# Moving the product of batch 0's last token row to other PSUM banks and an earlier place, and output copies behind the attention work, in a fused linear-attention and SwiGLU kernel

## The chip, the cores and the metric

The kernel runs on one core of a Trainium2 chip. The metric is the device time of one execution in microseconds (us).

## The reference

Linear attention with the feature map phi(x) = elu(x) + 1 on 8 batches, 8 heads, 576 tokens and head size 64, then a SwiGLU block on the 4608 x 512 result:

```
k.v = phi(k)^T v        z = sum over tokens of phi(k)
x   = (phi(q) k.v) / (phi(q) z + 1e-6)
out = (silu(x w_gate) * (x w_val)) w_out        # 512 -> 1536 -> 512
```

The kernel treats the 4608 tokens as nine groups of 512. A batch has 576 tokens, nine rows of 64, so group 0 holds eight rows of batch 0, and group 1 holds the ninth row of batch 0 and seven rows of batch 1.

## The kernel before

Names used below. PE is the matmul engine, ACT is ScalarE, DVE is VectorE, POOL is GpSimd. The granted clock is the share of its full clock that PE was allowed, as the trace records it (1 is full). The kernel uses eight PSUM banks: pG[0..1], pV[0..2], pX[0..2]. Each second-layer step of group 0 accumulates in pV[0], pG[0], pV[1] or pG[1]; between these steps the program interleaves the attention of batch 1 in the other four banks.

The pieces that matter, cut from the kernel (line numbers of the kernel before in comments; dots mark cuts; the lambdas of the list are left out):

```
def corners(ps, lhs, b, j0, j1, lps=(0, 1)):          # L260: one 64x64 matmul for each head
    for lp in lps:
        for hh in range(2):
            for e in range(2): nc.tensor.matmul(out=ps[2*lp+e][C*hh:C*hh+C, :], ...)

dbank, nbank = (pX[0], pX[1]), (pX[2], pV[2])

def t1(lp): ...        # L743: transposes of phi(q) of batch 1 into pX[0] (lp 0) or pX[2] (lp 1),
                       # copied out by ACT (lp 0, L746) or DVE (lp 1, L748)
def den1(lp):
    corners({2*lp+e: dbank[e][:, 0:W7] for e in range(2)}, zs, 1, 0, 7, (lp,))   # denominators
    ln0([b[:, 0:W7] for b in dbank], rr[:, 2*lp:2*lp+2, 0:W7])                     # L655: ACT, ln
    exp_neg(rr[:, 2*lp:2*lp+2, 0:W7])                                              # L658: 1/den

num8_out = [pV[2][:, 0:C], pX[1][:, W7:W7+C], pV[2][:, C:2*C], pX[0][:, W7:W7+C]]
def num8(): corners(num8_out, kv(0), 0, 8, 9)      # batch 0's ninth row times its k.v: 8 matmuls
def x8():                                          # L661: DVE, four small scalings of it
    for m in range(4): x0(num8_out[m], r8[:, m % 2, part8[m]], xT[m][1][:, 0:C])

w = at(17, [    # (step i, what): issued behind the i-th piece of group 0's second layer
    (3, z0(1,0)), (3, z0(1,1)), (3, q_block), (7, t1(0)), (8, t1(1)),
    (8, den1(0)), (8, num8), (8, x8), (9, mm1(1,0)), (9, mm1(1,1)),
    (9, den1(1)), (9, r1_copies), (10, num1(0)), (10, x1(0)), (10, w_rest),
    (12, t2), (12, num1(1)), (12, x1(1)), (13, exp_k(2,0)), (13, den2), (14, num2), ... ])

for (i, (t, f0, f1)) in enumerate(...):            # the 16 pieces of the second layer
    ...
    l2(0, t, f0, f1)                               # L446
    if i > 11: l2_out(0, t, V)                     # L456: DVE copies a finished output tile
    for f in w[i]: f()
```

z0 (L626) is the key sum of batch 1, mm1 (L177) its k.v product, num1 its numerators, t2 (L753, copied by DVE in L755) the transposes of its last two rows and den2 and num2 what num1 and den1 are for these two rows. `num8` is the subject. Its even corners go to pV[2], its odd ones to columns 448 to 511 of pX[1] and pX[0]. Columns 0 to 447 of these two banks are `den1`'s.

## Time and profile before

| | before |
|---|---|
| median time (range), as given with the kernel | 307.1 us (306.84 to 307.11), 3 runs |
| PE busy, mean granted clock | 97%, 0.996 (full in the stage; the recorded loss is in the last 2.4 us of the span, behind the last matmul) |
| stage studied: first second-layer matmul of group 0 to first first-layer matmul of group 1 | 36.57 to 53.34 = 16.77 us |
| PE's longest wait in that stage | 1.24 us |

The page of the kernel before, its busy times and its chain of work that ended last:

```profile
PE 296.4 (97%) x2596; PEld 181.5 (59%) x2596; DVE 247.5 (81%) x526; ACT 193.4 (63%) x313; POOL 49.2 (16%) x61
...
PE 89%; issue 5%; DMA 2%; ACT 1%; DVE 1%; POOL 0%; POOLq 0%; DVEq 0%; ACTq 0%
```

PE bounds the kernel. But the busy share says little of what is left to gain: the Trainium skill, "Trainium Kernel Development and Optimization", section "Performance Expectations", calls matmul busy time a bad metric for the distance to roofline because matmuls are pipelined. What can be gained are gaps between matmuls on the chain.

The timeline of PE in the kernel before (start, duration, instruction, shapes, count, and in brackets the idle time before it and what ended it):

```profile
42.02 0.55 PE L743 MATMUL pX<-id,qp 128*128 128x128 f16 x7
42.50 0.38 PE L260 MATMUL pX<-qT,zz 64*64 64x448 f16 x4
42.72 0.19 PE L260 MATMUL pV<-qT,R 64*64 64x64 f16 x1
44.14 0.19 PE L260 MATMUL pX<-qT,R 64*64 64x64 f16 x1 [1.24 <-ACT rr L655]
...
44.32 1.04 PE L446 MATMUL pG<-wo,hT 128*128 128x512 f16 x4
```

den1(0) is issued at 42.50. num8's first matmul, into pV, follows at 42.72. The second, into pX, starts only at 44.14. Everything behind it on PE, above all four ready second-layer matmuls, stands in the queue. The ACT timeline shows what it waits for, the two ln of den1(0):

```profile
42.93 1.16 ACT L655 ACTIVATE rr<-pX,epst 128x448 f32<-128x448 f32 x2 [0.66 <-PE pX L260]
```

They end at 44.09. num8 does not use their result. It only writes other columns of the two banks that they read. The skill, "PSUM — Partial Sum Buffer", section "Terms", says that a matmul writing a bank quadrant while ScalarE or VectorE reads it is a collision error; so the program has to order the two. The trace shows that ordering as a wait, and shows the first corner, in a bank that ACT does not read, passing freely.

A second, smaller gap, from the chain of the kernel before in order of time (start, duration, piece):

```profile
49.93 0.05 DVE osb L456
49.98 0.55 issue
50.53 0.42 DVE qT L755
50.96 0.04 issue
51.00 0.30 PE pX L260 x7
```

den2 at 51.00 waits for DVE's copy of the transposes t2 (L755), and that copy stood behind an output copy (L456). PE's last matmul before it started at 50.50; with a normal step of the size PE would have been free about 0.2 us before 51.00.

### The profile page before, as it was taken

To read this page: it belongs to the slowest core of one execution; us is meant where nothing else is said; L and a number is where in the kernel's file an instruction comes from. 1 tells how busy PE (TensorE), PEld (TensorE's weight loads), DVE (VectorE), ACT (ScalarE), POOL (GpSimd) and SP (SyncE) were. 2 spreads that over 40 slices of the span, in tenths; PEclk is the share of its full clock that TensorE was granted. 3 is DMA by queue.
4 is the path that set the end of the run, shared out by engine and by line. 5 is a ranking of instruction groups with operands and counts; after the bars stand their busy time and mean duration, and the time that the engine had idled before them with its cause. 6 is when DMAs were issued, how large, how long until landed. Compare 5 with 4: busy or idle time off the path is not lost.

```text
span 305.5 us, 6677 instructions
## 1 busy us (share of the span) xinstructions
PE 296.4 (97%) x2596; PEld 181.5 (59%) x2596; DVE 247.5 (81%) x526; ACT 193.4 (63%) x313; POOL 49.2 (16%) x61
## 2 busy tenths in 40 slices
PE   8899989999999999999999999999999999999993
PEld 5644444444444486447644774467446888878883
DVE  4754647888868997998899878997999868968991
ACT  4874976947754588466855685468633478547931
POOL 8654254510001001100110000000000004001300
PEclk9999999999999999999999999999999999999998
DMA  7999999999589218931794133133312050033014
GB/s 205 193 196 201 206 207 215 195 209 195 112 166 155 52 28 182 184 58 29 159 185 78 29 72 69 27 54 69 72 26 54 12 129 0 2 68 72 2 37 103
DMA packets 41472, 32.88 MB, mean 108 GB/s; under 512 B 16400, under 2 KB 36816, under 8 KB 41440
## 3 DMA queue, kind: packets, MB, share of 16 engines
q0 software_dynamic: 20176, 18.35, 38.6%
q1 hardware_dynamic: 21104, 13.97, 19.8%
q8 instruction: 20, 0.33, 0.4%
q10 hardware_dynamic: 160, 0.13, 0.2%
q14 instruction: 12, 0.10, 0.1%
HBM read 37.75 MB, written 9.44 MB: 154 GB/s over the span
## 4 chain that ended last, share of the span: by engine, by line
PE 89%; issue 5%; DMA 2%; ACT 1%; DVE 1%; POOL 0%; POOLq 0%; DVEq 0%; ACTq 0%
PE pV L287 23%; PE pG L287 21%; PE pX L502 14%; PE pV L502 4%; PE pV L339 4%; PE pG L339 4%; PE pV L446 3%; PE pX L287 3%; PE pG L446 3%; DMA q<-in_q_dram 2%; PE pV L260 1%; PE pX L260 1%; PE pX L339 1%; PE pX L177 1%; PE pV L407 1%
## 5 line engine op out<-in xcount | busy, mean ns | idle before, releaser
L287 PE MATMUL pV<-xT,wv 128*128 128x512 f16 x324 | 83.5, 379 | 0.0
L287 PE MATMUL pG<-xT,wg 128*128 128x512 f16 x296 | 76.3, 379 | 0.0
L292 ACT ACTIVATE sil<-pG 128x512 f16<-128x512 f32 x74 | 43.5, 597 | 47.1 <-PE pG L287 32.2
L293 DVE SCALAR_TENSOR_TENSOR hT<-pV,sil 128x512 f16<-128x512 f32 x81 | 55.0, 687 | 15.2 <-PE pV L287 7.6
L287 PEld LDWEIGHTS <-wv 128*128 128x128 f16 x336 | 32.9, 98 | 39.6
L287 PEld LDWEIGHTS <-wg 128*128 128x128 f16 x336 | 32.3, 98 | 39.1 <-DVE xT L276 0.8
L502 PEld LDWEIGHTS <-hs 128*128 128x128 f16 x336 | 32.5, 98 | 4.7 <-DVE hs L476 0.4
L379 POOL TENSOR_TENSOR hT<-prod,vm 128x512 f16<-128x512 f16 x6 | 6.9, 1153 | 127.5 <-ACT vm L366 127.5
L502 PEld LDWEIGHTS <-hT 128*128 128x128 f16 x252 | 24.3, 98 | 4.1
L502 PE MATMUL pX<-ws,hs 128*128 128x256 f16 x210 | 25.7, 273 | 0.0
L507 ACT ACTIVATE part<-pX 128x256 f32<-128x256 f32 x35 | 12.8, 381 | 13.2 <-PE pX L502 13.1
L476 DVE TENSOR_TENSOR hs<-hT 128x512 f16<-128x512 f16 (+2 forms) x42 | 17.4, 417 | 0.2
L241 DVE TENSOR_TENSOR qp<-qp,rden 128x768 f16<-128x768 f16 x18 | 17.1, 948 | 0.0
L228 DVE TENSOR_REDUCE den<-prod 128x12 f32<-128x768 f16 x18 | 17.0, 942 | 0.0
L120 ACT ACTIVATE ek<-k 128x1152 f16<-128x1152 f16 x14 | 16.0, 1160 | 0.1
L95 POOL DMA_DIRECT2D k<-in_k_dram x7 | 5.2, 745 | 64.1 <-ACT part L507 44.0
L502 PE MATMUL pX<-wo,hT 128*128 128x256 f16 x126 | 15.2, 272 | 0.0
L130 DVE TENSOR_TENSOR kp<-kp,ek 128x1152 f16<-128x1152 f16 x14 | 10.6, 758 | 5.4 <-ACT ek L120 5.0
L446 PEld LDWEIGHTS <-hT 128*128 128x128 f16 x96 | 8.7, 98 | 10.1 <-issue 0.6
L151 ACT ACTIVATE vm<-v 128x1152 f16<-128x1152 f16 x12 | 14.1, 1175 | 0.0
L120 ACT ACTIVATE eq<-q 128x1152 f16<-128x1152 f16 x12 | 13.3, 1169 | 0.0
L512 DVE SCALAR_TENSOR_TENSOR osb<-pX,part 128x256 f32<-128x256 f32 x28 | 11.0, 418 | 2.1 <-PE pX L502 1.9
(186 smaller groups left out, 514.7 us busy)
## 6 DMA issues: line engine op xcount, KB each, us to landing
out_dram<-osb SPq DMA_DIRECT2D x64, 128.0 KB, 2.6
k<-in_k_dram POOLq DMA_DIRECT2D x7, 576.0 KB, 7.6
q<-in_q_dram POOLq DMA_DIRECT2D x7, 576.0 KB, 9.3
v<-in_v_dram POOLq DMA_DIRECT2D x7, 576.0 KB, 12.1
wg<-in_moe_w_gate_dram POOLq DMA_DIRECT2D x5, 256.0 KB, 8.9
wv<-in_moe_w_val_dram POOLq DMA_DIRECT2D x5, 256.0 KB, 9.5
wo<-in_moe_w_out_dram POOLq DMA_DIRECT2D x2, 512.0 KB, 15.1
out_dram<-osb SPq DMA_DIRECT2D x13, 64.0 KB, 2.0
```

The source lines that it names most:

```text
L120: nc.scalar.activation(out=e[:, s, :], in_=src[b % 2][:, s, :], func=AF.Exp, bias=0.0, scale=1.0)
L151: nc.scalar.activation(out=vm[b % 2][:, :, s, 0:D].rearrange("p j l d -> p l j d"), in_=v16[b % 2][:, s, :].rearrange("p l (j d) -> p l j ...
L228: nc.vector.tensor_reduce(out=den[:, HL * j0:HL * j1], in_=prod[:, 0:j1 - j0, :].rearrange("p j (l d) -> p (j l) d", d=D), axis=AX.X, op=A ...
L241: nc.vector.tensor_tensor(out=qv, in0=qv, in1=rden[:, HL * j0:HL * j1].unsqueeze(2).to_broadcast([P, HL * (j1 - j0), D]), op=ALU.mult)
L287: nc.tensor.matmul(out=ps[:, :], lhsT=src[:, i, P * fb:P * fb + P], rhs=xT[i][g % 2][:, :], start=(i == 0), stop=(i == 3))
L292: nc.scalar.activation(out=s[:, :], in_=pg[:, :], func=AF.Silu, bias=0.0, scale=1.0)
L293: nc.vector.scalar_tensor_tensor(out=hT[g % 2][:, fb, :], in0=pv[:, :], scalar=SC, in1=s[:, :], op0=ALU.mult, op1=ALU.mult)
L339: nc.tensor.matmul(out=dst[:, HN * e:HN * e + HN], lhsT=lhs, rhs=rhs, start=(n in (1, 2, 5) and e == 0 and c == 0), stop=(c == 1), skip_gr ...
L446: nc.tensor.matmul(out=pso[(g, t)][:, :], lhsT=hT[g % 2][:, fb, P * t:P * t + P], rhs=wo[:, fb, :], start=(fb == 0), stop=(fb == FB - 1))
L476: (eng or nc.vector).tensor_tensor(out=o, in0=a, in1=b, op=op)
L502: nc.tensor.matmul(out=(z if n in (2, 3, 5) else x)[:, 0:HD], lhsT=left(f), rhs=right(f), start=(f == 0 and n in (1, 2, 5)), stop=(f == HF ...
L507: nc.scalar.activation(out=part[:, 2 * i + tt, :], in_=(x if from_x else z)[:, 0:HD], func=AF.Copy, bias=0.0, scale=1.0 / SC)
```

## The change

The intent is to give num8 banks that nobody reads at the moment when it is issued, and to let PE go straight from den1(0) to second-layer matmuls while ACT takes the ln. num8 goes to step 3, in front of the key sums z0, into the free last 128 columns of the two banks of z0. Its scalings x8 go behind the q block. Apart from that, the output copies are issued behind the step's attention work.

```diff
-    num8_out = [pV[2][:, 0:C], pX[1][:, W7:W7 + C], pV[2][:, C:2 * C], pX[0][:, W7:W7 + C]]
+    num8_out = [(pX[2], pV[2])[m % 2][:, 3 * P:4 * P][:, part8[m]] for m in range(4)]
...
-            (3, lambda: z0(1, 0)), (3, lambda: z0(1, 1)), (3, q_block), (7, lambda: t1(0)), (8, lambda: t1(1)),
-            (8, lambda: den1(0)), (8, lambda: num8()), (8, lambda: x8()), (9, lambda: mm1(1, 0)), (9, lambda: mm1(1, 1)),
+            (3, lambda: num8()), (3, lambda: z0(1, 0)), (3, lambda: z0(1, 1)), (3, q_block), (3, lambda: x8()), (7, lambda: t1(0)), (8, lambda: t1(1)),
+            (8, lambda: den1(0)), (9, lambda: mm1(1, 0)), (9, lambda: mm1(1, 1)),
...
         l2(0, t, f0, f1)
+        for f in w[i]:
+            f()
         if i > 11:
             l2_out(0, t, V)
-        for f in w[i]:
-            f()
```

## The prediction

> **What bounds it.** The matmul engine (PE): the page gives 97% busy, 89% of the chain that ended last, granted clock 0.996. Busy time is a poor distance to the roofline (the Trainium skill, "Trainium Kernel Development and Optimization", Performance Expectations), so I looked for PE gaps. In the timeline of group 0's second layer (36.6 to 53.3 us) the last-row product num8 issues its first matmul, into pV, at 42.72; its second, into pX, starts only at 44.14. The waits view has PE pX <- ACT rr (ln), 1.24 us, PE's only listed wait there. The ln reads other columns of the same pX banks; the first matmul, in a bank that ACT does not read, went through. That agrees with the skill ("PSUM — Partial Sum Buffer", Terms): PE writing a bank while ScalarE reads it is a collision, so the program waits. It is in the chain ("ACT rr 1.16, issue 0.04").
>
> A small second gap: chain "DVE osb 0.05, issue 0.55, DVE qT 0.42, issue 0.04" before den2 at 51.00. PE would be free at about 50.82. The copy of the transposes stood behind an output copy (0.68 us, DVE).
>
> **The change.** It computes the same. num8's eight matmuls (0.18 us on PE) move to step 3, before z0, into columns 384 to 511 of pX[2]/pV[2], banks that z0 waits for there anyway. Its four scalings x8 (DVE, 0.61 us together) move behind the q block. Output copy 0 goes behind the transposes' copy and x1(1).
>
> **Walk of the new schedule** (estimates from the durations above):
> - PE after step 3 runs 0.2 us later: t1(1) at 42.2, den1(0) at 42.7.
> - x8 on DVE 41.3 to 41.9 (the last minimum ends at 41.38), before t1(1) overwrites pX[2]: no new wait, 0.3 us of slack.
> - Four second-layer matmuls follow den1(0) at once (43.0), then mm1 at 44.0. v of batch 1 landed at 43.5: 0.5 us of slack, the tightest transfer.
> - den1(1) at 44.6; the ln it must wait for ends at 44.3. PE has useful work for the length of the ln.
> - num1(0) 45.85; t2 47.9; its copy on DVE 48.5 to 48.9; den2 at 49.5 without a wait.
> - exp of batch 2's k stays at 48.4: its load lands only then (31.4 plus 17.0). It ends at 49.55, just before ln of den2 wants ACT (49.85).
> - First layer of group 1 starts at about 51.9 instead of 53.34.
>
> So 1.24 + 0.17 + about 0.1 of saved array switches, about 1.5 us, all on the critical path. After that PE is nearly gapless to the end, ACT and DVE shift along, and later loads land early enough, so nearly all should survive: 307.1 - 1.5 = 305.6 us.
>
> **Predicted: 305.6 us, range 305.0 to 306.4; faster by over 2%: 0.01, within 2%: 0.98, slower: 0.01.** A gain of 0.5%.
>
> **Signs.** Right if: the 1.24 us wait is gone; num8 appears at 38.4; no wait of 0.1 us or more before mm1 or den1(1); group 1's first layer starts 1.3 to 1.6 us earlier; later stages keep their lengths.
>
> **What would make it wrong.** (1) mm1 waits for v's landing, or ACT, late with exp of k, holds ln of den2 and so num2: gain 0.5 to 1. (2) den1(1) waits for the ln after all (0.3 us margin). (3) x8 late on DVE holds t1(1). (4) Group 1's first layer waits for ACT's table load and silu: gain given back. (5) Run to run spread (before: 0.27 us).

## The result, and the profile after

After: 305.61 us median (305.19 to 305.71, 4 runs), beside 306.97 us (306.84 to 307.11, 4 runs) of before. The ratio is 0.9953, 95% interval 0.9936 to 0.997. A ratio here is the mean time of one kernel's runs over that of the other's of the same rounds, so not quite the ratio of the quoted medians. In a second set of rounds, below as `after_again`, it was 0.9955 (305.74 beside 307.15).

PE in the kernel after, the answer to the lines shown of before:

```profile
37.83 0.21 PE L260 MATMUL pX<-qT,R 64*64 64x64 f16 x1
...
41.64 0.55 PE L743 MATMUL pX<-id,qp 128*128 128x128 f16 x7
42.13 0.38 PE L260 MATMUL pX<-qT,zz 64*64 64x448 f16 x4
42.44 1.04 PE L446 MATMUL pG<-wo,hT 128*128 128x512 f16 x4
...
48.93 0.31 PE L260 MATMUL pX<-qT,zz 64*64 64x128 f16 x8
49.17 1.04 PE L446 MATMUL pV<-wo,hT 128*128 128x512 f16 x4
```

num8 now runs at 37.83. From the transposes at 41.64 to the next second-layer matmuls at 42.44 it is 0.80 us, where it was 2.30 (42.02 to 44.32). den2 (48.93) and the four matmuls behind it carry no wait. The chain in order of time has PE alone here, no ACT and no DVE:

```profile
41.81 0.39 PE pX L743 x7
42.20 0.31 PE pX L260 x4
42.51 0.97 PE pG L446 x4
43.48 0.15 PE pX L177 x2
...
48.03 0.97 PE pG L446 x4
49.00 0.24 PE pX L260 x8
49.24 0.97 PE pV L446 x4
```

The gain is small, but both intervals exclude 1.

Where the time went, from the starts of PE's matmuls in the two traces:

| stretch of PE | before | after | difference |
|---|---|---|---|
| stage studied | 16.77 us | 15.27 us | -1.50 |
| of it: last matmuls of step 3, over z0 (and num8), to the next piece | 1.16 | 1.34 | +0.18 |
| of it: transposes t1(1) to the next piece | 2.30 | 0.80 | -1.50 |
| of it: piece ahead of den2 to the piece behind it | 1.39 | 1.20 | -0.19 |
| group 1's first layer, to its second layer | 22.03 | 22.02 | -0.01 |
| from there to the last matmul | 225.11 | 225.11 | 0.00 |

The stage keeps its 1.50 us and the rest of the kernel neither adds nor gives back. The profiled executions differ by more, 305.5 to 303.4 us, because the second one also reached the stage 0.56 us earlier (36.01 against 36.57). The change touches nothing that early, and in other executions the stage begins anywhere from 35.90 to 36.74 us. That start is the larger part of the noise of the totals: from the start of the stage to the end of the span, `after` and `after_again` differ by only 0.03 us. It is no gain of the change.

### The profile page after: what moved, and what is told of

It is laid out like the page before. It is cut to its first block, busy times and chain, and to the rows that moved or that the text cites. A ratio compares the mean times of both kernels' runs of the same rounds, so it can differ in the third digit from the quotient of the medians.

```text
span 303.4 us, 6676 instructions
## 1 busy us (share of the span) xinstructions
PE 295.6 (97%) x2596; PEld 181.0 (60%) x2596; DVE 247.6 (82%) x526; ACT 193.1 (64%) x313; POOL 49.2 (16%) x61
## 4 chain that ended last, share of the span: by engine, by line
PE 89%; issue 4%; DMA 2%; ACT 1%; DVE 1%; POOL 0%; POOLq 0%; DVEq 0%; ACTq 0%
PE pV L287 23%; PE pG L287 21%; PE pX L502 14%; PE pV L502 4%; PE pV L339 4%; PE pG L339 4%; PE pG L446 4%; PE pV L446 4%; PE pX L287 3%; DMA q<-in_q_dram 2%; PE pV L260 1%; PE pX L260 1%; PE pX L339 1%; PE pX L177 1%; PE pV L407 1%
```

## The experiments

The theory: PE's wait lasts as long as some engine reads the bank that num8 writes. The gain is that wait (1.24 us and 0.08 of what went with it) plus the separate gap before den2 (0.18). The rivals: the place in the order counts and the bank does not; any bank away from the ln is enough; the order of the output copies did most of it by making room on DVE; the end of the wait was a coincidence with something else, such as a load.

All results, with the stage length of each profile. Totals are medians, and each ratio is to the kernel before in the same rounds.

| run | stage, us | PE's longest wait in the stage | time, us (before) | ratio, 95% interval |
|---|---|---|---|---|
| before | 16.77 | 1.24 for ACT | | |
| after | 15.27 | none | 305.61 (306.97) | 0.9953, 0.9936 to 0.997 |
| e1_num8_only | 15.45 | 0.12, den2 | 305.84 (306.89) | 0.9965, 0.9953 to 0.9978 |
| e2_copies_only | 16.59 | 1.24 for ACT | 306.71 (306.89) | 0.9994, 0.9982 to 1.0007 |
| e3_bank_only | 15.93 | 0.40 for DVE | 306.08 (306.89) | 0.9974, 0.996 to 0.9988 |
| e4_place_only | 16.44 | 0.84 for DVE | 306.63 (306.89) | 0.9991, 0.9979 to 1.0004 |
| e5_dose_before | 18.92 | 1.90 for ACT | 309.12 (307.12) | 1.0056, 1.0033 to 1.0079 |
| e6_dose_after | 15.70 | 0.08 inside den1(1) | 305.79 (307.12) | 0.9954, 0.994 to 0.9969 |
| e8_half_dose | 17.23 | 1.69 for ACT | 307.57 (307.15) | 1.0009, 0.9997 to 1.0022 |
| e7_phi_q_later | 15.27 | none | 305.33 (307.12) | 0.9938, 0.9924 to 0.9952 |
| after_again | 15.27 | none | 305.74 (307.15) | 0.9955, 0.9941 to 0.9968 |
| e7_again | 15.27 | none | 305.33 (307.15) | 0.9938, 0.9926 to 0.9951 |

### e1: num8's move alone

The kernel after, with the old order of the output copies:

```diff
         l2(0, t, f0, f1)
-        for f in w[i]:
-            f()
         if i > 11:
             l2_out(0, t, V)
+        for f in w[i]:
+            f()
```

> The move of num8 and x8 (bank and place) without the new order of output copies. Measured by the stage length, from the first second-layer matmul of group 0 to the first first-layer matmul of group 1: 16.77 us before, 15.27 after. Theory (two separate terms): the 1.24 us wait on ln is gone, den2 still waits for the transposes' copy behind output copy 0, so the stage is 15.4 to 15.5 us and the time 1.2 us under before. Rival (the output copies' order made room on DVE, and the move alone gains little): stage above 16 us.

Stage 15.45 us, 1.32 less than before: as expected. The time was 1.05 us under before, a little less than the 1.2 expected. The gap before den2 was still there (0.12 us idle, for DVE's copy L755). DVE's timeline shows why, the output copy stands in front:

```profile
48.77 0.68 DVE L456 TENSOR_SCALAR osb<-pV 128x512 f32<-128x512 f32 x1
49.38 0.41 DVE L755 COPY qT<-pX 128x512 f16<-128x512 f16 x1
```

### e2: the order of the output copies alone

The kernel before with only the last part of the change:

```diff
         l2(0, t, f0, f1)
+        for f in w[i]:
+            f()
         if i > 11:
             l2_out(0, t, V)
-        for f in w[i]:
-            f()
```

> Only the new order of output copies, num8 as before. Theory: only the gap before den2 closes: stage 16.55 to 16.65 us against 16.77 (0.15 to 0.2 less), the 1.24 us wait on ln unchanged; in the total hardly to be told from noise. Rival (the order of copies is the larger part): stage under 16.2 us.

Stage 16.59 us, 0.18 less, and the wait for ln is still 1.24 us. In the total it can't be told from noise, as expected. 1.32 and 0.18 make 1.50: the two parts add up exactly, and they are independent.

### e3: other banks, old place

```diff
-    num8_out = [pV[2][:, 0:C], pX[1][:, W7:W7 + C], pV[2][:, C:2 * C], pX[0][:, W7:W7 + C]]
+    num8_out = [(pX[2], pV[2])[m % 2][:, 3 * P:4 * P][:, part8[m]] for m in range(4)]
```

A first form with all four corners in pV[2], where nobody reads, has no run: matmuls of two row tiles (the even and the odd corners) write one bank with nothing to order them. The skill says the same ("TensorEngine Tiling (Array Packing)", section "Gotcha 1: PSUM Pressure": different row tiles can't access the same bank at once); no run here shows it on the chip. So num8 needs two banks, and at its old place there was no second free one.

> num8 stays at its old place behind den1(0); only its two banks change to pX[2] and pV[2]. At that moment no ln reads them, but VectorE's copy of the transposes reads pX[2] until about 43.2 us of the before trace. Theory (the wait is for whoever reads the bank that is written): the wait on ACT is gone and a shorter one on VectorE's copy (L748) takes its place, about 0.5 us; stage 15.9 to 16.2 us. Rival A (it waits for data, or for the place in the order, not for the bank): wait about 1.24 us as before, stage 16.7 to 16.8. Rival B (any bank away from ln is enough): no wait, stage 15.4 to 15.6.

```profile
42.20 0.38 PE L260 MATMUL pX<-qT,zz 64*64 64x448 f16 x4
42.99 0.19 PE L260 MATMUL pX<-qT,R 64*64 64x64 f16 x1 [0.40 <-DVE qT L748]
```

The wait is not gone and not 1.24 us. It is 0.40 us and it is for DVE's copy of the transposes, which reads pX[2]. The wait follows the reader of the bank. That rules out rival A, a wait for data or for a coincidental event at 44.1 us, and rival B.

### e4: new place, old banks

num8 at step 3 and x8 behind the q block, as in the change, with the old order of output copies; but the odd corners stay in den1's banks:

```diff
-    num8_out = [(pX[2], pV[2])[m % 2][:, 3 * P:4 * P][:, part8[m]] for m in range(4)]
+    num8_out = [pV[2][:, 3 * P:3 * P + C], pX[1][:, W7:W7 + C], pV[2][:, 3 * P + C:4 * P], pX[0][:, W7:W7 + C]]
```

> num8 at the new early place with x8 behind the q block, but its pX halves stay in den's banks pX[0] and pX[1] (columns 448 to 511); output copies as before. Theory: nobody reads these banks when num8 is issued, so it does not wait; but the transposes t1(0) now write pX[0] and must wait for the last x8 (end at about 41.3 to 41.4 in the after trace, t1(0) came at 40.4): a wait of about 1.0 us on VectorE at t1(0), stage 16.3 to 16.6 us, so most of the gain is lost. Rival (the early place is what counts, the bank does not matter): stage 15.4 to 15.5.

PE's timeline of e4:

```profile
40.46 0.59 PE L446 MATMUL pG<-wo,hT 128*128 128x512 f16 x2
41.89 0.55 PE L743 MATMUL pX<-id,qp 128*128 128x128 f16 x7 [0.84 <-DVE xT L661]
```

The last of x8's four scalings, on DVE, ends just before:

```profile
41.62 0.22 DVE L661 SCALAR_TENSOR_TENSOR xT<-pX,r 128x64 f16<-128x64 f32 x1
```

num8 itself no longer waits. But t1(0), which writes pX[0] next, must wait until x8 has read num8's corner from that bank. That costs 1.00 us from start to start (1.43 between the two lines, where two matmuls take 0.43), and 1.32 of gain less 1.00 leaves 0.32; the stage is 0.33 shorter than before. The place alone keeps a quarter of what e1 gains. Neither the place nor the banks alone make the gain: a bank must be free of readers when num8 writes it, and read out before the next writer wants it.

### e5 and e6: a longer ln

In both kernels the first ln of den1(0) is done twice, which changes no result:

```diff
+        if lp == 0:
+            ln0([dbank[0][:, 0:W7]], rr[:, 0:1, 0:W7])
         ln0([b[:, 0:W7] for b in dbank], rr[:, 2 * lp:2 * lp + 2, 0:W7])
```

> The kernel before with the first ln of den1(0) done twice (same result): one more read of pX[0] by ACT, about 0.55 us, ahead of the end of ln. Theory: num8's wait grows by all of it, from 1.24 to about 1.8 us, stage 16.77 to about 17.3 us. Rival (the wait is fixed by something else that ends at the same time, such as a load's landing): the wait stays 1.24, stage 16.8.

```profile
44.66 0.19 PE L260 MATMUL pX<-qT,R 64*64 64x64 f16 x1 [1.90 <-ACT rr L655]
```

The wait grew as the theory says, from 1.24 to 1.90 us; the extra ln cost 0.66, more than the estimated 0.55. But the stage grew by 2.15 us, not by 0.5. The missing 1.49 us are no wait. The table of stretches of e5 shows them (start and end, length, then busy us and count of instructions of PE, PEld, DVE, ACT and POOL, then granted clock, DMA share, GB/s; PEld is PE's weight load):

```profile
42.60:44.60 2.00, 0.16 (x5) 0.00 (x0) 0.49 (x1) 1.78 (x3) 2.00 (x2) 1.00 1.23 206
45.20:48.60 3.40, 3.40 (x82) 1.53 (x80) 0.85 (x5) 1.07 (x3) 0.72 (x1) 0.50 1.21 208
48.80:52.00 3.20, 3.20 (x24) 1.34 (x22) 2.33 (x5) 2.29 (x3) 0.00 (x0) 1.00 1.21 207
```

After the wait the granted clock was 0.50 for 3.4 us (45.2 to 48.6), with 512-column matmuls 427 ns apart where they are 216 ns apart elsewhere. Three of the four runs have mean clock 0.994 and lie 1.9 to 2.6 us over the median of before. Only one of the three left a trace; for the other two the half clock is inferred from these numbers. The fourth has clock 1.000 and lies only 0.65 us over it, about what the longer wait alone costs; it left no trace. So the same edit did not always bring the half clock; e8 says more on when.

> The same extra ln in the kernel after. Theory: PE does second-layer matmuls and mm1 behind the ln and reaches den1(1) about 0.3 us after the ln ends (44.00 against 43.71), so 0.3 of the 0.55 us is hidden and a new wait of about 0.25 us appears at den1(1); stage 15.27 to about 15.5 us. Rival (no slack: ACT's chain now bounds the stage): stage grows by 0.5 us or more; rival (ACT far off the path): stage unchanged.

ACT's three ln took 1.82 us in place of 1.16, so the dose was again 0.66. The stage grew by 0.43 us, so 0.23 of it was hidden: that is the slack between the end of ln and den1(1). It is near the 0.3 us of the prediction; the stage itself came out longer than the 15.5 expected because the dose was larger. den1(1)'s first corner, in pX[0], went at 44.16 (first line, from PE's timeline); the second, in pX[1], started 0.43 us behind it, when the last ln had ended (the others, from the chain):

```profile
44.16 0.81 PE L260 MATMUL pX<-qT,zz 64*64 64x448 f16 x4
...
43.38 1.17 ACT rr L655 x2
44.55 0.04 issue
44.59 0.38 PE pX L260 x3
```

The order fits the theory once more: the extra ln and the first regular one read pX[0], only the last reads pX[1]. So the change has turned the wait into a slack of about a quarter of a microsecond, not into a large one.

### e8: half the dose

As e5, with an extra ln over 192 columns:

```diff
+        if lp == 0:
+            ln0([dbank[0][:, 0:3 * C]], rr[:, 0:1, 0:3 * C])
         ln0([b[:, 0:W7] for b in dbank], rr[:, 2 * lp:2 * lp + 2, 0:W7])
```

> The kernel before with an extra ln over 192 instead of 448 columns in den1(0). The full dose made PE idle for 1.90 us and was followed, in the three of its four runs whose mean clock was 0.994, by 3.41 us at half clock; the fourth run had clock 1.000 and lost only the 0.66 us of wait. Theory (the clock halves when enough of some window of about 3.4 us is idle): ln of 192 columns is about 0.42 us (estimate from 0.47 for 256 and 0.63 for 448), so the wait is about 1.65 to 1.7 us, just under half of 3.41, and the clock stays: stage 17.2 us, time 0.45 us over before, no run at clock 0.994. Rival (any wait over about 1.3 us can trigger it): some runs at 0.994 and 1.9 us over before.

```profile
44.31 0.19 PE L260 MATMUL pX<-qT,R 64*64 64x64 f16 x1 [1.69 <-ACT rr L655]
```

The wait was 1.69 us, the stage 17.23, no run had a clock under 0.997, and the time was 0.42 us over before. So 0.45 us more of wait cost 0.42 us in the total; 0.66 us more (e5) cost 1.9 to 2.6 us in three runs of four. The kernel before, with 1.24 us, showed no half clock in the stage in its trace.

The clock records of the traces tell more. In every kept trace the stretches of full clock last a whole number of steps of 3.413 us: in e5 40.96 us, which is 12 steps, from 4.27 us to the drop at 45.23; in before 296.96 us, 87 steps. In e8 the record of full clock begins at 4.29 us, so its 12th step ends at 45.25. In both, this 12th step contains the whole wait. It and the step behind it, in e5 and then in e8:

```profile
41.82:45.23 3.41, 1.51 (x23) 0.86 (x21) 0.90 (x4) 2.69 (x5) 3.33 (x4) 1.00 1.23 206
45.23:48.64 3.41, 3.41 (x82) 1.53 (x80) 0.82 (x5) 1.08 (x3) 0.69 (x1) 0.50 1.21 207
```

```profile
41.84:45.25 3.41, 1.72 (x24) 0.86 (x21) 1.24 (x5) 2.68 (x5) 3.33 (x4) 1.00 1.23 206
45.25:48.66 3.41, 3.41 (x91) 1.63 (x90) 1.32 (x4) 2.16 (x4) 0.34 (x1) 1.00 1.21 208
```

With PE busy for 1.51 us of the step the next one ran at half clock, with 1.72 us it did not. The other steps of the twelve kept traces fit. Those with less PE work (1.38 us at the end of e1, 1.40 at the end of e2, and less or none at the other ends) were followed by half clock; those with more (1.67 us at the end of e6, all others 2.4 and up) by full clock. The closest is at the end of e5: 1.53 us, and no half clock. So in these traces PE's busy time within a step separates the two cases, with a limit near 1.5 of 3.41 us; the ends of matmuls are modelled, so it is no sharper than that. It is not shown that e5's fourth run escaped because a step ended inside its wait. In the trace of before one does (at 43.67), which splits its 1.24 us.

### e7 and after_again: a further step

After the change one PE gap is left behind the start-up: the matmul zb of batch 2. By the chain of the kernel after, it is again a wait for a reader of a bank: zb writes pX[0], ACT's copies of R (L192) read pX[0], and they follow four small DVE instructions (zd, L185) that stand behind the second half of batch 2's q features. But zb also needs the result of zd, so this experiment, which moves both, does not tell the bank from the data. The edit of the kernel after lets zd go first:

```diff
-                     (2, lambda: phi_q(2, 1)), (3, lambda: joint(2))] + items
+                     (3, lambda: joint(2)), (3, lambda: phi_q(2, 1))] + items
```

> The kernel after, with the second half of batch 2's q features on VectorE moved behind batch 2's joint step. In the after trace the matmul zb at 62.73 us starts 0.27 us later than PE could (0.49 us from the matmul before it to it, against 0.22 between matmuls of that size), behind VectorE's zd. Theory: zd comes over 1 us earlier, this gap closes, 0.15 to 0.27 us less in the stretch from group 1's first layer to its second layer (22.02 us in the after trace, 22.03 before), nothing new elsewhere: about 0.2 us less than after in total, hardly above noise. Rival: ACT's or VectorE's queue is held elsewhere and the stretch is the same or longer.

PE in the kernel after, then in e7:

```profile
61.59 1.03 PE L287 MATMUL pV<-xT,wv 128*128 128x512 f16 x4
62.73 0.38 PE L208 MATMUL pX<-zd,ones 128*128 128x512 f16 x1
```

```profile
61.74 1.03 PE L287 MATMUL pV<-xT,wv 128*128 128x512 f16 x4
62.61 0.38 PE L208 MATMUL pX<-zd,ones 128*128 128x512 f16 x1
```

From the four matmuls to zb it is 1.14 us in the first and 0.87 in the second. The stretch is 21.75 us in place of 22.02. For a fair comparison the kernel after and this one ran once more on one chip:

> The kernel after unchanged, to stand beside the next run on one chip. Stage 15.27 us, time 1.3 to 1.5 us under before (ratio 0.9950 to 0.9960).

> The kernel with the later q features once more (it was 305.33 us beside 307.12 of before, with the stretch of group 1's first layer at 21.75 instead of 22.02 us). Theory: 0.27 us under the kernel after in the same rounds. Rival (its 305.33 was a lucky chip): the same as after.

Medians 305.74 and 305.33 us. The stretch of e7 was 21.75 us again, so the 0.27 us of the trace are solid. The intervals of the two ratios overlap (0.9941 to 0.9968 and 0.9926 to 0.9951), so the total alone does not settle it. This version is clear of the kernel before, and under the kernel after by what the trace shows.

## Why the prediction was right

Predicted 305.6 us (305.0 to 306.4); measured 305.61. That the totals agree to 0.01 us is partly luck: the prediction took 1.5 us from 307.1, while before had 306.97 in the rounds of the result, so the total fell by 1.36 us (1.41 in the second set). The length of the stage, 1.50 us less, is what confirms the sum. Point by point:

- **The main term.** Predicted: the 1.24 us wait and about 0.1 of array switches. Measured with e1: 1.32 us. e3, e4 and e5 show that the wait is one for the reader of the bank. That the 0.08 on top of the wait are array switches was only argued; e1 shows the sum.
- **The small term.** Predicted 0.17; e2 measured 0.18.
- **num8's place.** Predicted at 38.4 in a trace whose stage begins at 36.57, so 1.83 us into the stage; it came 1.82 us in (37.83 less 36.01), and cost PE the 0.18 us there that it had cost before.
- **v's load.** Predicted slack 0.5 us. In the after trace v was issued at 26.38 and landed 16.6 us later, at 42.97; mm1 began at 43.40, so the slack was 0.43. A weight load is listed as having waited for it (first line below), but PE shows no gap there: the chain has mm1 directly behind the matmuls ahead of it.
- **exp of batch 2's k.** Predicted: it can't move, because its load lands only at 48.4. It did wait for the load, 1.14 us, and ended in time: ACT was idle for 0.26 us before the ln of den2. From the waits of the kernel after:

```profile
PEld L177 <- DMA v<-in_v_dram: 0.4, 1, 0.4
ACT ek L120 <- DMA k<-in_k_dram: 1.1, 1, 1.1
```

- **den1(1) and the ln.** Predicted margin 0.3 us; e6 measured 0.23.
- **Nothing given back.** Predicted that nearly all survives; the stretches behind the stage are the same to 0.01 us.

What the prediction did not see: how near the wait was to one that brings half the clock with it (e5), and that the total of a pair of single runs carries a start-up difference of up to 0.8 us.

## What to carry to other kernels

When PE waits for an engine whose result it does not use, ask which PSUM bank the two share, columns or not; give the small product a bank that is free when it is written and read out before the next writer, because a free bank at the wrong place (e3) or the right place in a busy bank (e4) only moves the wait to another instruction. Pieces that have to wait anyway, here den1(1) for ln, should have ready matmuls in front of them. When a gain is under 1%, compare the lengths of a stage in the traces, and use totals as a check.

## What the Trainium skill lacked or had wrong

- "TensorE: Matmul & The Clock Gate", "Part 1: The HAM clock gate" and "HAM oscillation", ties the drop to half clock to an idle window or gap of about 3.4 us (a further section, on PSUM-queue cycling, has frequent short idle times bring it too, but gives no length). Here a PE wait of 1.90 us, with work before and behind it, was followed by 3.413 us at clock 0.50 (e5): PE had been busy for 1.51 us, 44%, of the 3.41 us step before the drop. With 1.72 us, 50%, there was none (e8), and the twelve kept traces put the limit near 1.5 us, far from a step without work. Of e5's four runs, three were 1.9 to 2.6 us slower than before and one only 0.65. Waits of 1.24 and 1.69 us showed nothing of it. The length of the slow stretch agrees with the page's window of 3413 ns.
- "PSUM — Partial Sum Buffer" describes a shared bank as an error. No page says what avoiding it costs in a tuned schedule; here 1.24 us of PE for a product of 0.18 us, from an ln on other columns of the bank.
